# Attention and token mixing on one core: wq and mixing on halves of 288 tokens, bias products 2048 wide, a new order

## The chip, the cores and the metric

One Trainium2 chip, one of its cores. The metric is device microseconds of the whole kernel on that core, the median of several runs. One execution was also taken with the hardware profiler; its trace gives the start and end of every instruction on TensorE (PE), VectorE (DVE), ScalarE (ACT), GpSimd (POOL) and SyncE (SP), and of every DMA.

## What is computed

Eight batches, eight heads, 576 tokens, 64 columns a head. First, attention over a window of 128 tokens with a linear distance bias; then its output, with the heads side by side, is x [576, 512] per batch, and goes through a token mixing layer. q, k, v, the weights and the output are float32 in memory.

```
scores = q @ k^T / 8;  bias = -slope[h] * |i - j|          # 0 <= i - j < 128, else masked
x = softmax(scores + bias) @ v                             # [8, 576, 512]
wq = x @ w_q;  wk = x @ w_k                                # [8, 576, 64]
W_tok = wq @ wk^T / 8
out = relu(W_tok @ x) @ w_out                              # [8, 576, 512]
```

## The kernel before

Every batch goes through the same steps, each a function that the kernel calls once per piece. In the names below b is the batch.

Loads: Lq, Lk (q and k of four heads or of 128 tokens), Lt (the last 64 tokens of two batches), Lv (v of 128 tokens), Lwq, Lwk, Lwo (weights). They stand on POOL's queue and cast to 16 bits (helper line 220); each waits until the loads issued some 6 us of transfer before it have landed (lines 368 to 380). The first half of q comes over SP in 32 bits (FQ) and is cast on an engine (CQ).

Attention: TW, TN and TT transpose q and k on PE into the tile qkT (helper line 217), and ETW, ETN and ETT copy them from PSUM (lines 492, 494, 235, 237). QK{b}.{g}.{u} computes the scores of key group g (128 keys, the last group 192) for four heads u. EXP (line 604, ACT) takes the exponential of 1024 columns from two PSUM banks into the tile pt; MUL (line 611, DVE) multiplies them by the exponential of the bias, which holds the mask too. There are 64 of each. PV{b}.{qt} multiplies by v, with a column of ones for the sum, and X (lines 649 and 650, DVE: a reciprocal and a product) normalises into x; the last 64 tokens of a batch go into xtl.

Mixing: XT transposes x, and EXT copies it (lines 235, 237) into two tiles xT of 256 tokens and a padded one, xTt, of the last 64. WQ computes wq^T from 128 columns of weights, in which the 64 columns of w_q stand twice (tile wqq_sb), so that rows 0 to 63 and 64 to 127 of wqT both hold wq^T: steps .0 and .1 for 256 tokens each, .2 for 64, and EWQ copies each (lines 229, 231). WK gives wk, EWK copies it. G is wk^T x, 64 x 512: columns 0 to 255 of x on one half of the array's columns and 256 to 511 on the other, so that the tile gs holds two halves on rows 0 to 63 and 64 to 127. MX{b}.0 and .1 multiply G^T by wq^T: two matmuls of 512 tokens, each on one half of the array's rows, side by side; .2 does the last 64 tokens in four matmuls. RM is the relu with a scale (line 750 ACT, 752 DVE), per 512 columns, and one of 256 for the tails. OUT multiplies by w_out, four matmuls of 512 columns for 128 tokens; OUT{b}.4, for odd b, does the tails of two batches at once. EO copies the result (229, 231), DO stores it, on POOL or SP (line 223).

All matmuls are recorded at line 214, and all copies at 229, 231, 235 and 237. An array shape stands in the trace as 128*128, 64*128 (row halves) or 128*64 (column halves).

PSUM is four tiles of two banks ("pair"). The order of the work is a table, ORDER: words `name:engine:bank:fills`, from first to last; every engine runs its own words strictly in that order, and waits at a word for what it needs. The fourth field puts that many matmuls on zeros (tile fill, 512 columns) ahead of a step. HOLD marks the place from which stores on SP wait for the last load.

```
EXP0.0.0:A QK0.2.1:P:1:3 QK0.0.1:P:2 QK0.1.1:P:0 MUL0.0.0:V Lv0.1:G EXP0.1.1:A TT0:P:3
...
    for word in ORDER.split():
        name, eng, *rest = word.split(":")
        op = ops.pop(name)
        op.eng = ENG[eng]
...
            op.fill = int(rest[1]) if len(rest) > 1 else 0
```

## Time and profile before

| | before |
|---|---|
| median of 3 runs | 137.87 us (137.78 to 138.77) |
| span of the profiled execution | 137.4 us |
| PE busy | 127.2 us (93%), 2364 matmuls |
| PE weight loads | 83.5 us (61%) |
| DVE busy | 112.0 us (82%), 236 instructions |
| ACT busy | 113.8 us (83%), 187 instructions |
| POOL busy | 105.3 us (77%), 170 instructions |
| mean granted clock of PE | 0.983 |
| last bias product ends | 117.2 us |
| last work of PE | up to 132.5 us |

The profiled execution is one run of its own; its span goes from the first to the last instruction of the core. "Busy" counts an engine's instructions, not its waits, and a busy PE includes the fills. The profile also follows the chain of work that ended last: 72% of the span on PE, 8% on ACT, 5% on loads.

### The profile page before, as it was taken

What the parts mean: (1) busy time and instruction counts of PE and PEld (TensorE: products, weight loads), DVE (VectorE), ACT (ScalarE), POOL (GpSimd) and SP (SyncE); (2) the same over time, 40 slices, a digit from 0 to 9 for tenths busy, and PEclk for the clock granted to TensorE, in tenths of its full rate; (3) what the DMA queues carried; (4) which work ended last, traced back from release to release, by engine and by line L of the source; (5) the groups of instructions that cost most, each with busy time, mean ns of one, the idle gap of its engine ahead of it and who ended that gap; (6) DMA issues with size and microseconds to landing.
All of it is one profiled execution on the core that took longest, in us unless ns stands there. A gap on an engine that the chain in (4) does not pass through costs nothing.

```text
span 137.4 us, 5570 instructions
## 1 busy us (share of the span) xinstructions
PE 127.2 (93%) x2364; PEld 83.5 (61%) x2364; DVE 112.0 (82%) x236; ACT 113.8 (83%) x187; POOL 105.3 (77%) x170
## 2 busy tenths in 40 slices
PE   6997599979999999999999999999999999999950
PEld 2363366778676575667657766766668784765410
DVE  4437838999899999999999999999998899973700
ACT  3769559999979988999989999999999999543750
POOL 6999984899999899999999999999998810100110
PEclk9999959999999999999999999999999999999998
DMA  4999999999999999999999999999999990399994
GB/s 131 162 155 166 158 169 174 181 137 138 135 180 143 163 155 152 149 140 130 143 141 147 149 142 146 140 135 150 198 258 268 342 328 21 115 357 339 329 299 172
DMA packets 92680, 24.86 MB, mean 181 GB/s; under 512 B 80240, under 2 KB 89200, under 8 KB 92656
## 3 DMA queue, kind: packets, MB, share of 16 engines
q0 software_dynamic: 89488, 19.28, 150.0%
q1 hardware_dynamic: 3168, 5.24, 10.8%
q8 instruction: 18, 0.29, 0.8%
q14 instruction: 6, 0.05, 0.1%
HBM read 29.62 MB, written 9.44 MB: 284 GB/s over the span
## 4 chain that ended last, share of the span: by engine, by line
PE 72%; ACT 8%; DMA 5%; POOL 5%; issue 3%; DVE 2%; POOLq 0%; DVEq 0%
PE pair L214 62%; PE pair L217 10%; DMA natw<-in_k_dram 5%; ACT pt L604 5%; POOL natt L220 2%; POOL natw L220 2%; ACT qkT L492 2%; DVE x L650 1%; DVE xtl L650 1%; DVE xT L237 1%; DVE inv L649 0%; ACT xT L235 0%; ACT osb L229 0%; ACT wqT L229 0%; POOL wm L293 0%
## 5 line engine op out<-in xcount | busy, mean ns | idle before, releaser
L604 ACT ACTIVATE pt<-pair 128x1024 f16<-128x1024 f32 x64 | 63.3, 1038 | 6.0 <-PE pair L214 5.8
L220 POOL DMA_DIRECT2D vt<-in_v_dram x40 | 36.5, 968 | 1.2 <-DMA natw<-in_k_dram 0.8
L611 DVE TENSOR_TENSOR pt<-pt,bias 128x1024 f16<-128x1024 f16 x48 | 32.2, 684 | 1.4 <-ACT pt L604 1.3
L214 PE MATMUL pair<-wout_sb,rm 128*128 128x512 f16 x128 | 32.0, 380 | 0.1
L223 POOL DMA_DIRECT2D out_dram<-natw x19 | 10.6, 566 | 19.5 <-DVE natw L231 10.9
L214 PEld LDWEIGHTS <-pt 128*128 128x128 f16 x576 | 21.2, 98 | 5.5 <-issue 2.2
L214 PE MATMUL pair<-qkT 64*128 64x256 f16 (+3 forms) x352 | 23.8, 247 | 0.4 <-ACT pt L604 0.3
L214 PE MATMUL pair<-vt,pt 128*128 128x65 f16 x576 | 23.8, 194 | 0.1
L220 POOL DMA_DIRECT2D natw<-in_k_dram x24 | 22.9, 993 | 1.2 <-POOLq L894 0.8
L220 POOL DMA_DIRECT2D natw<-in_q_dram x23 | 21.5, 989 | 2.0 <-DMA natw<-in_k_dram 0.7
L650 DVE TENSOR_TENSOR x<-pair,inv 128x512 f16<-128x512 f32 x32 | 22.1, 692 | 1.1
L214 PEld LDWEIGHTS <-rm 128*128 128x128 f16 x128 | 10.8, 97 | 10.9 <-issue 0.9
L214 PEld LDWEIGHTS <-qkT 64*128 64x128 f16 x352 | 11.9, 96 | 7.7 <-issue 3.9
L229 ACT COPY natw<-pair 128x512 f32<-128x512 f32 x24 | 14.1, 607 | 2.2 <-PE pair L214 2.1
L217 PEld LDWEIGHTS <-natw 128*64 128x64 f16 (+1 forms) x512 | 12.8, 103 | 4.8 <-issue 1.9
L214 PE MATMUL pair<-fill 128*128 128x512 f16 x28 | 10.4, 506 | 1.2 <-DVE fill L348 1.2
L750 ACT ACTIVATE rm<-pair 128x512 f16<-128x512 f32 x20 | 11.4, 611 | 0.0
L611 DVE TENSOR_TENSOR pt<-pt,biasl 128x1024 f16<-128x1024 f16 x16 | 10.9, 683 | 0.0
L217 PE MATMUL pair<-permh,natw 128*64 128x128 f16 x256 | 9.1, 223 | 1.8 <-DMA natw<-in_k_dram 1.4
L649 DVE RECIPROCAL inv<-pair 128x8 f32<-128x8 f32 (+1 forms) x40 | 8.1, 203 | 3.1 <-PE pair L214 2.3
L214 PE MATMUL pair<-xT,wqq_sb 128*128 128x256 f16 x64 | 9.3, 273 | 0.4 <-ACT qkT L492 0.4
L752 DVE TENSOR_SCALAR rm<-pair 128x512 f16<-128x512 f32 x12 | 7.9, 684 | 1.6 <-PE pair L214 1.6
(76 smaller groups left out, 178.2 us busy)
## 6 DMA issues: line engine op xcount, KB each, us to landing
vt<-in_v_dram POOLq DMA_DIRECT2D x32, 128.0 KB, 5.1
out_dram<-natw POOLq DMA_DIRECT2D x15, 256.0 KB, 5.0
out_dram<-natw SPq DMA_DIRECT2D x13, 256.0 KB, 3.1
natw<-in_k_dram POOLq DMA_DIRECT2D x8, 256.0 KB, 5.6
natw<-in_q_dram POOLq DMA_DIRECT2D x16, 128.0 KB, 5.0
natw<-in_k_dram POOLq DMA_DIRECT2D x16, 128.0 KB, 5.2
natw<-in_q_dram POOLq DMA_DIRECT2D x7, 256.0 KB, 6.0
out_dram<-osb SPq DMA_DIRECT2D x3, 256.0 KB, 3.5
```

The source lines that it names most:

```text
L214: hold(nc.tensor.matmul(*a, **k))
L217: hold(nc.tensor.transpose(*a))
L220: hold(nc.gpsimd.dma_start(**k))
L223: i = (nc.gpsimd if eng == "POOL" else nc.sync).dma_start(**k)
L229: hold(nc.scalar.copy(out_ap, in_ap))
L492: hold(nc.scalar.copy(dst, src))
L604: nc.scalar.activation(out=pt[:, 0:1024], in_=two(s.bank).rearrange("p e c -> p (e c)"), func=AF.Exp, scale=SCALE)
L611: nc.vector.tensor_tensor(out=pt[:, 0:1024], in0=pt[:, 0:1024], in1=bt, op=ALU.mult)
L649: nc.vector.reciprocal(out=inv[r], in_=pxv[r, :, :, 64])
L650: nc.vector.tensor_tensor(out=x[r].rearrange("p (g h d) -> p g h d", g=2, h=4), in0=pxv[r, :, :, 0:64], in1=inv[r].unsqueeze(3).broadcast_ ...
L750: hold(nc.scalar.activation(out=out_ap, in_=in_ap, func=AF.Relu, scale=WSCALE))
L752: hold(nc.vector.tensor_scalar(out=out_ap, in0=in_ap, scalar1=0.0, scalar2=WSCALE, op0=ALU.max, op1=ALU.mult))
```

## The change

1. WQ{b} is one step. It uses the 64 columns of w_q as they are, on column halves: tokens 0 to 287 on one half, 288 to 575 on the other, eight matmuls of 288 columns. wqT then has 288 columns with the token halves on rows 0 to 63 and 64 to 127. It needs all three transposes of x (EXT). The doubled weights and their copy go.
2. G is computed as before, and copied twice: EG into gs as it is, and GX into gx with its halves exchanged (two copies of 64 rows), on ACT in batches 0 and 3, on DVE in batch 7, and by two SP transfers of 64 x 256 elements, from gs, in batches 1, 2, 4, 5 and 6. MX has four steps of two matmuls of 288 columns, on row halves; .2 and .3 use gx. RM takes 2 x 288 columns per step: 32 relus of 576 columns instead of 32 of 512 and 8 of 256. OUT{b}.4 uses column halves, one per batch.
3. xT is one tile of 576 tokens, so that its padded tail tile goes; xtl has four buffers and only their unused halves are set to zero.
4. In batches 1 to 7 one bias product covers both groups of heads, 2048 columns, and waits for both exponentials; batch 0 keeps eight products of 1024. In all 36 products instead of 64.
5. The order is a new one. Fills: 10, all ahead of the first transposes, instead of 28. Several memsets move (ones2, ones4, zerop and pads from POOL to DVE, zerop with five memsets instead of ten), and the casts of the first q are both on DVE. HOLD stands near the end. The helpers' lines shift: 214 is now 207 (matmul), 217 is 210, 604 is 590, 611 is 603, 750 and 752 are 757 and 759.

Words per engine that change most: EO on ACT 27 to 22, on DVE 9 to 14; EXT on ACT 12 to 19, on DVE 12 to 5; RM on ACT 25 to 23, on DVE 15 to 9; EWQ on ACT 14 to 4, on DVE 10 to 4; copies of transposed q and k on ACT 27 to 20, on DVE 13 to 20; DO on POOL 18 to 20, on SP 18 to 16.

```diff
+HS = 288
...
+WIDE = (1, 2, 3, 4, 5, 6, 7)
+DUO = ()
+HW = 2
-PTW = 1088
+PTW = 2112
...
 ORDER = """
-CQ0:V CQ1:A Lt0.2:G zeros:V bias0:A idh:V Lt0.1:G perm:V TW0.0:P:0:12 Lt0.0:G biasl0:V
+Lt0.1:G Lt0.0:G CQ0:V ones2:V CQ1:V perm:V bias0:A TW0.0:P:0:10 ETW0.0.0:A Lt0.2:G zeros:V
...
-    wqq_sb = sb("wqq_sb", [P, 4, P], F16)
...
-    pt_s = [[sb(f"pt{i}{u}", [P, PTW], F16) for u in range(2)] for i in range(NPT)]
+    pt_s = [sb(f"pt{i}", [P, PTW], F16) for i in range(NPT)]
...
-    xT_s = [[sb(f"xT{i}{n}", [P, 4, 256], F16) for n in range(2)] for i in range(2)]
-    xTt_s = [sb(f"xTt{i}", [P, 4, P], F16) for i in range(2)]
-    wqT_s = [sb(f"wqT{i}", [P, S], F16) for i in range(2)]
+    xtl_s = [sb(f"xtl{i}", [P, DM], F16) for i in range(4)]
+    xT_s = [sb(f"xT{i}", [P, 4, S], F16) for i in range(2)]
+    wqT_s = [sb(f"wqT{i}", [P, HS], F16) for i in range(2)]
...
-    rm_s = [[sb(f"rm{i}{c}", [P, DM], F16) for c in range(4)] for i in range(2)]
-    rmt_s = [sb(f"rmt{i}", [P, 4, P], F16) for i in range(2)]
+    gx_s = [sb(f"gx{i}", [P, 256], F16) for i in range(2)]
+    rm_s = [sb(f"rm{i}", [P, 2, 8, HS], F16) for i in range(2)]
...
         x = add(f"EXP{b}.{g}.{u}", ACT(0.905), [s, *oldp], ex, frees=[s])
-        bt = (bias if g < 3 else biasl)[u].rearrange("p e a c -> p (e a c)")
+        wide = b in WIDE
+        exps[b, g, u] = x
+        if wide and u == 0:
+            return
+        us = (0, 1) if wide else (u,)
+        lo, hi = 1024 * us[0], 1024 * us[-1] + 1024
 
         def ml(o):
-            nc.vector.tensor_tensor(out=pt[:, 0:1024], in0=pt[:, 0:1024], in1=bt, op=ALU.mult)
-
-        mul[b, g, u] = add(f"MUL{b}.{g}.{u}", DVE(0.6), [x, (mkb if g < 3 else mkl)[u]], ml)
+            bt = biasw[g == 3].rearrange("p u e a c -> p (u e a c)")
+            nc.vector.tensor_tensor(out=pt[:, lo:hi], in0=pt[:, lo:hi], in1=bt[:, lo:hi], op=ALU.mult)
+
+        m = add(f"MUL{b}.{g}" + ("" if wide else f".{u}"), DVE(1.13 if wide else 0.6),
+                [exps[b, g, v] for v in us] + [(mkb if g < 3 else mkl)[v] for v in us], ml)
+        for v in us:
+            mul[b, g, v] = m
 
...
-    def add_wq(b, i):
-        n = 64 if i == 2 else 256
-
-        def em(o):
-            pw = one(o.bank)
...
+    def add_wq(b):
+        def em(o):
             for c in range(4):
-                rhs = xT_s[b % 2][i][:, c, :] if i < 2 else xTt_s[b % 2][:, c, 64 * (b % 2):64 * (b % 2) + 64]
-                mm(pw[:, 0:n], wqq_sb[:, c, :], rhs, start=(c == 0), stop=(c == 3))
-
-        t = add(f"WQ{b}.{i}", pe(0.436 if i < 2 else 0.116), [wts[0], ext[b, i]], em, banks=1)
-        wqd[b, i] = t
+                for r in range(2):
+                    mm(one(o.bank)[64 * r:64 * r + 64, 0:HS], wq_sb[:, c, :],
+                       xT_s[b % 2][:, c, HS * r:HS * r + HS], start=(c == 0), stop=(c == 3))
+
+        t = add(f"WQ{b}", pe(0.5), [wts[0], *[ext[b, i] for i in range(3)]], em, banks=1, mode=2)
+        wqd[b] = t
 
         def ev(o):
-            cp(o.eng, wqT_s[b % 2][:, 256 * i:256 * i + n], one(t.bank)[:, 0:n])
-
-        old = [mxd.get((b - 2, j)) for j in range(3)]
-        ewq[b, i] = add(f"EWQ{b}.{i}", EV(0.26, 0.34) if i < 2 else EV(0.11, 0.14), [t, *old], ev, frees=[t],
-                        group=f"w{b}")
+            cp(o.eng, wqT_s[b % 2], one(t.bank)[:, 0:HS])
+
+        old = [mxd.get((b - 2, j)) for j in range(4)]
+        ewq[b] = add(f"EWQ{b}", EV(0.292, 0.367), [t, *old], ev, frees=[t])
 
...
-        old = [mxd.get((b - 2, j)) for j in range(3)]
-        egs[b] = add(f"EG{b}", EV(0.26, 0.34), [g, *old], evg, frees=[g])
+        old = [mxd.get((b - 2, j)) for j in range(2)]
+        egs[b] = add(f"EG{b}", EV(0.265, 0.333), [g, *old, gxs.get(b - 2)], evg, frees=[g])
+
+        def evx(o):
+            for r in range(2):
+                out_ap = gx_s[b % 2][64 * r:64 * r + 64, :]
+                lo = slice(64 - 64 * r, 128 - 64 * r)
+                if o.eng == "SP":
+                    hold(nc.sync.dma_start(out=out_ap, in_=gs_s[b % 2][lo, :]))
+                elif o.eng == "POOL":
+                    hold(nc.gpsimd.tensor_copy(out=out_ap, in_=gs_s[b % 2][lo, :]))
+                else:
+                    cp(o.eng, out_ap, one(g.bank)[lo, 0:256])
+
+        old = [mxd.get((b - 2, j)) for j in range(2, 4)]
+        gxs[b] = add(f"GX{b}", {**EV(0.53, 0.666), "POOL": (0.6, 0.65), "SP": (0.9, 0.9)}, [g, egs[b], *old], evx, frees=[g])
 
...
     def add_mix(b, j):
-        g, w = gs_s[b % 2], wqT_s[b % 2]
+        g, w = (gs_s, gx_s)[j // 2][b % 2], wqT_s[b % 2]
 
         def em(o):
             pm = two(o.bank)
-            if j < 2:
-                for r in range(2):
-                    h = slice(64 * r, 64 * r + 64)
-                    mm(pm[:, r, :], g[h, P * j:P * j + P], w[h, 0:512], start=True, stop=True)
+            for r in range(2):
+                h = slice(64 * r, 64 * r + 64)
+                mm(pm[:, r ^ (j // 2), 0:HS], g[h, P * (j % 2):P * (j % 2) + P], w[h, :], start=True, stop=True)
+
+        t = add(f"MX{b}.{j}", pe(0.125, 0.1), [(egs, gxs)[j // 2][b], ewq[b]], em, banks=2, mode=1)
+        mxd[b, j] = t
+        old = [osd.get((b - 4, st)) for st in range(4)]
+        old += [osd.get((b // 2 * 2 - 3, 4))]
+
+        def ev(o):
+            c, n = (2 * j, 5) if j < 2 else (2 * j - 3, 3)
+            relu(o.eng, rm_s[(b // 2) % 2][:, b % 2, c:c + n + 1:n, :], two(t.bank)[:, :, 0:HS])
+
+        erm[b, j] = add(f"RM{b}.{j}", EV(0.532, 0.667), [t, *old], ev, frees=[t], group=f"rm{b}")
+
+    def add_out(b, st):
+        duo = b in DUO and st < 4
+        head = outd.get((b, st - 1)) if duo and st % 2 else None
+
+        def em(o):
+            if head:
+                o.bank = head.bank
+            po = two(o.bank)[:, st % 2, :] if duo else one(o.bank)
+            rm = rm_s[(b // 2) % 2].rearrange("p b c t -> p b (c t)")
+            for db in range(4):
+                if st < 4:
+                    lo = 2 * HS * db + P * st + 64 * (st // 2)
+                    mm(po, rm[:, b % 2, lo:lo + P], wout_sb[:, db, :], start=(db == 0), stop=(db == 3))
+                else:
+                    for e in range(2):
+                        lo = 2 * HS * db + 256
+                        mm(po[64 * e:64 * e + 64], rm[:, e, lo:lo + 64], wout_sb[:, db, :], start=(db == 0), stop=(db == 3))
+
+        need = [*wto]
+        need += [erm[b, db] for db in range(4)]
+        if st == 4:
+            need += [erm[b - 1, db] for db in range(4)]
+        if head:
+            need.append(head)
+        t = add(f"OUT{b}.{st}", pe(0.865, 0.2), need, em, banks=0 if head else 2 if duo else 1, mode=0 if st < 4 else 2)
+        outd[b, st] = t
+        osd[b, st] = t
...
```

PE, the start, before: weight loads and matmuls by turns; the last scores of a step of batch 0 (from qkT_80, its transposed q and k), a fill, and the first transpose of batch 1 (natw_83 is loaded q or k of batch 1, pair_n a PSUM tile).

```order
L214 LDWEIGHTS qkT_80
L214 MATMUL pair_191<-qkT_80 128x256
L214 LDWEIGHTS fill
L214 MATMUL pair_189<-fill 128x512
L217 LDWEIGHTS natw_83
L217 MATMUL pair_189<-permh,natw_83 64x32x4
```

PE, the same place, after: (qkT_77 is the transposed q and k of batch 0, natp_79 loaded q or k of batch 1).

```order
L207 LDWEIGHTS qkT_77
L207 MATMUL pair_159<-qkT_77 128x256
L210 LDWEIGHTS natp_79
L210 MATMUL pair_160<-permh,natp_79 64x32x4
L210 LDWEIGHTS natp_79
```

The fill is gone, and the scores ahead are other ones: the last of key groups 3 and 1 (QK0.3 and QK0.1.1), of which QK0.3 stood behind these transposes before.

ACT, the start, before: constants, then copies of transposed q and k (L492, L235) and exponentials (L604) of batch 0, and from qkT_81 on of batch 1.

```order
L305 ACTIVATE bias_72<-wm 128x256 x4
L492 COPY qkT_80<-pair_189 128x2x256
L604 ACTIVATE pt_147<-pair_190 128x1024
L604 ACTIVATE pt_145<-pair_191 128x1024
L492 COPY qkT_80<-pair_189 128x2x256
L604 ACTIVATE pt_143<-pair_192 128x1024
L604 ACTIVATE pt_146<-pair_189 128x1024
L604 ACTIVATE pt_148<-pair_190 128x1024
L604 ACTIVATE pt_144<-pair_191 128x1024
L235 COPY qkT_80<-pair_192 128x8x32
L604 ACTIVATE pt_149<-pair_190 128x1024
L492 COPY qkT_81<-pair_189 128x2x256 x2
```

ACT, the start, after: the same steps, L478 and L228 for the copies and L590 for the exponentials; qkT_78 is batch 1.

```order
L478 COPY qkT_77<-pair_157 128x2x256
L590 ACTIVATE pt_125<-pair_157 128x1024
L478 COPY qkT_77<-pair_160 128x2x256
L590 ACTIVATE pt_124<-pair_158 128x1024
L590 ACTIVATE pt_124<-pair_157 128x1024
L228 COPY qkT_78<-pair_158 128x8x32
L228 COPY qkT_77<-pair_158 128x8x32
L590 ACTIVATE pt_126<-pair_160 128x1024
L590 ACTIVATE pt_126<-pair_159 128x1024
L590 ACTIVATE pt_127<-pair_157 128x1024
L590 ACTIVATE pt_125<-pair_160 128x1024
L590 ACTIVATE pt_127<-pair_158 128x1024
```

One exponential instead of two stands ahead of the copy of the transposed heads 4 to 7 (the second row with qkT and a PSUM tile of 128x2x256), and all eight exponentials of batch 0 but none of batch 1 stand ahead of the copy of transposed batch 1 of the kind 128x2x256.

DVE, batch 2, before: relus, products (L611), normalisations (L649, L650) and copies.

```order
L611 TENSOR_TENSOR pt_151<-pt_151,bias_72 128x1024
L611 TENSOR_TENSOR pt_146<-pt_146,biasl_75 128x1024
L611 TENSOR_TENSOR pt_145<-pt_145,biasl_74 128x1024
L649 RECIPROCAL inv<-pair_191 128x8
L650 TENSOR_TENSOR x_154<-pair_191,inv 128x512
L611 TENSOR_TENSOR pt_147<-pt_147,bias_72 128x1024
L611 TENSOR_TENSOR pt_149<-pt_149,bias_72 128x1024
L649 RECIPROCAL inv<-pair_192 128x8
L650 TENSOR_TENSOR x_155<-pair_192,inv 128x512
```

DVE, batch 2, after: products are L603, normalisations L644 and L645, copies L224 and L480.

```order
L644 RECIPROCAL inv<-pair_158 128x8
L645 TENSOR_TENSOR x_130<-pair_158,inv 128x512
L224 CAST gs_148<-pair_159 128x256
L603 TENSOR_TENSOR pt_124<-pt_124,bias_72 128x2048
L603 TENSOR_TENSOR pt_125<-pt_125,bias_73 128x2048
L480 TENSOR_SCALAR qkT_78<-pair_157 128x2x256
L644 RECIPROCAL inv<-pair_159 128x8
L645 TENSOR_TENSOR x_131<-pair_159,inv 128x512
L644 RECIPROCAL inv<-pair_158 128x8
L645 TENSOR_TENSOR x_132<-pair_158,inv 128x512
```

A product covers 2048 columns where it covered 1024, and two tiles stand for four.

321 lines of the change are left out of this document (142 added, 179 removed).

## The prediction

> **What bounds the kernel now.** I read the span by stages first, cutting it at the last bias product (117.1 us) and at the end of TensorE's work, then the grouped durations of ScalarE and VectorE, then the timeline at the start and at the end. The columns: stretch, length, busy time (and instructions) of PE, PEld, DVE, ACT and POOL, granted clock, share of the DMA engines, GB/s.
>
> ```profile
> 0.00:9.00 9.00, 7.81 (x55) 3.33 (x57) 4.20 (x22) 4.95 (x11) 7.68 (x17) 1.00 0.99 153
> 9.00:37.00 28.00, 24.55 (x521) 17.70 (x518) 21.99 (x46) 24.58 (x34) 24.63 (x52) 0.94 1.68 155
> 37.00:117.10 80.10, 79.54 (x1610) 53.80 (x1607) 76.45 (x150) 75.62 (x125) 71.31 (x101) 1.00 1.88 170
> 117.10:132.50 15.40, 15.35 (x192) 8.68 (x188) 9.37 (x20) 8.07 (x19) 1.63 (x3) 1.00 0.81 286
> ```
>
> From 37 to 117.1 us three engines are nearly full: TensorE 79.54 of 80.10 (99.3%), VectorE 95.4%, ScalarE 94.4%. TensorE alone is the bound there, with the two others five per cent behind; a gain on it is worth only as much as the next engine lets through. From 117.1 to 132.5 TensorE is full alone. Only before 37 us does it wait. So the sum has four terms: the start, the middle, the stretch behind the last product, the last stores.
>
> **What the change takes from TensorE.** The unit prices, from start to start:
>
> ```profile
> 102.94 0.66 PE L214 MATMUL pair<-vt,pt 128*128 128x65 f16 x16
> 103.46 0.60 PE L214 MATMUL pair<-xT,wqq_sb 128*128 128x256 f16 x4
> 103.89 0.65 PE L214 MATMUL pair<-vt,pt 128*128 128x65 f16 x16
> ...
> 105.24 0.29 PE L214 MATMUL pair<-xTt,wqq_sb 128*128 128x64 f16 x4
> 105.37 0.63 PE L214 MATMUL pair<-wk_sb,xT 128*128 128x64 f16 x16
> ```
>
> ```profile
> 107.77 0.63 PE L214 MATMUL pair<-x,wkn 128*64 128x256 f16 x8
> 108.23 0.28 PE L214 MATMUL pair<-xtl,wkn 128*64 128x256 f16 x2
> 108.44 0.72 PE L217 MATMUL pair<-identh,x 64*128 64x64 f16 x32
> ```
>
> ```profile
> 95.64 1.04 PE L214 MATMUL pair<-wout_sb,rm 128*128 128x512 f16 x4
> 96.51 0.65 PE L214 MATMUL pair<-vt,pt 128*128 128x65 f16 x16
> ...
> 97.65 1.04 PE L214 MATMUL pair<-wout_sb,rm 128*128 128x512 f16 x4
> 98.62 0.26 PE L214 MATMUL pair<-qkT 64*128 64x192 f16 x2
> ```
>
> A whole wq step of four matmuls lasts 103.89 - 103.46 = 0.43 us, the tail's four 0.13 us: 0.99 us per batch. An output step lasts 0.87 us when the next one has the same array shape (96.51 - 95.64) and 0.97 when it has another (98.62 - 97.65), so a change of shape costs 0.10. G, five pairs of matmuls on column halves, takes 0.67 with that 0.10 in it, or 0.114 per pair of 256 columns: the two halves do run side by side. The new wq step is four such pairs of 288 columns, 4 x 0.114 x 288/256 = 0.51 us. That saves 0.48 per batch, 3.8 us over eight. Counted in the instruction order, the shape changes go from 118 to 119 (+0.1); the last output step of a batch pair on column halves costs nothing much (+0.1 for four). Mixing streams 2 x 512 + 128 columns per row half before and 4 x 288 = 1152 after: nothing. TensorE's work without fills falls by 3.6 us.
>
> [...]
>
> Not all of it falls ahead of the last product. Behind that product the list of TensorE held 11 output steps, 4 value steps, 4 wq and 4 mixing steps; now 13, 2, 1 and 7, with ten shape changes for six. By the prices above (value step 0.52, from 102.94 to 103.46; a mixing step 0.12 where it was 0.22, or 0.06 for a tail): +1.74 - 1.04 - 0.61 + 0.30 + 0.40 = +0.8 us for the stretch behind the last product, so TensorE's work in the middle falls by 4.4, to 75.1 us.
>
> **ScalarE and VectorE in the middle.** Here busy time divided by the count is the price, since neighbours overlap a little.
>
> ```profile
> L604 ACT ACTIVATE pt<-pair 128x1024 f16<-128x1024 f32 x64 | 63.3, 1038 | 6.0 <-PE pair L214 5.8
> L229 ACT COPY natw<-pair 128x512 f32<-128x512 f32 x24 | 14.1, 607 | 2.2 <-PE pair L214 2.1
> L750 ACT ACTIVATE rm<-pair 128x512 f16<-128x512 f32 x20 | 11.4, 611 | 0.0
> L235 ACT COPY qkT<-pair 128x512 f32<-128x512 f32 x10 | 5.8, 593 | 0.7 <-ACT wqT L229 0.4 <-PE pair L214 0.3
> ...
> L229 ACT CAST wqT<-pair 128x256 f16<-128x256 f32 x9 | 3.4, 402 | 0.0
> ```
>
> ```profile
> L611 DVE TENSOR_TENSOR pt<-pt,bias 128x1024 f16<-128x1024 f16 x48 | 32.2, 684 | 1.4 <-ACT pt L604 1.3
> ...
> L752 DVE TENSOR_SCALAR rm<-pair 128x512 f16<-128x512 f32 x12 | 7.9, 684 | 1.6 <-PE pair L214 1.6
> L649 DVE RECIPROCAL inv<-pair 128x8 f32<-128x8 f32 x32 | 6.5, 203 | 3.0 <-PE pair L214 2.3
> ```
>
> Counting words of the order up to the last exponential, ScalarE loses five output copies (5 x 0.59 = 2.9), three 512-column and four 256-column transposes (3 x 0.58 + 4 x 0.36 = 3.2), a wk copy and the start's cast (1.1), and its wq copies go from nine of 256 and three of 64 columns to three of 288 (-2.9). It gains five wide and two small copies of xT (+3.5), two copies of G and four half-copies for the swapped G (+2.2), and its relus go from 14 of 512 and 3 of 256 columns to 20 of 576 (+3.0). Sum -1.4, of it 0.6 in the start: 75.62 falls to 74.9 us in the middle. The 64 exponentials, 63.3 us, stay.
>
> VectorE: 64 products become 8 + 28. No wide product stands in the trace. It has as many elements as the two that it replaces, so it saves at least 0 and at most a whole short instruction, the 203 ns of the reciprocal of 8 elements a partition. I take 70 ns, a tenth of a product's 684: 28 x 0.07 = 2.0, bounds 0 and 5.7. Six fewer relus and seven fewer xT copies at 0.68 (-8.8) and six fewer wq copies at some 0.4 (-2.4) stand against five more output copies and six more qkT copies at 0.68 (+7.5). In all 5.7 us less: some 71 us of work in the middle, and not the bound. A product that waits for both exponentials is ready one exponential later than the first of two was, 0.99 us; the value steps behind it in TensorE's list are kept further behind in the new order, and the five buffers of exponentials hide it.
>
> So after the change TensorE holds 75.1 us of work in the middle and ScalarE 74.9: they are level. Neither can be as full as TensorE was alone. Between ScalarE's present share, 94.4%, and TensorE's, 99.3%, I take the middle, 97%: 74.9 / 0.97 = 77.2 us against 80.1, -2.9. Ends: 75.1 / 0.993 = 75.6 (-4.5) and 74.9 / 0.944 = 79.3 (-0.8).
>
> **The start.**
>
> ```profile
> 9.57 1.08 PE L217 MATMUL pair<-permh,natw 128*64 128x128 f16 x32
> ```
>
> ```profile
> 9.14 1.94 ACT L604 ACTIVATE pt<-pair 128x1024 f16<-128x1024 f32 x2 [0.93 <-PE pair L214]
> ...
> 18.87 1.02 ACT L604 ACTIVATE pt<-pair 128x1024 f16<-128x1024 f32 x1 [3.18 <-PE pair L214]
> ```
>
> ```profile
> L220 POOL DMA_DIRECT2D vt<-in_v_dram x40 | 36.5, 968 | 1.2 <-DMA natw<-in_k_dram 0.8 <-DMA natw<-in_q_dram 0.4
> ```
>
> ```profile
> 13.70:17.20 3.50, 2.07 (x41) 1.32 (x41) 2.95 (x6) 2.00 (x3) 3.43 (x7) 0.95 2.08 163
> 17.20:20.60 3.40, 3.38 (x56) 2.24 (x53) 1.14 (x3) 1.73 (x3) 2.92 (x5) 0.55 1.72 168
> ```
>
> ScalarE idles 3.18 us before 18.87, because TensorE's list holds the transposes of batch 1 ahead of the scores of the fourth key block. The new order puts those scores first, and that wait goes. A new one comes: the second exponential stands behind the copy of the transposed heads 4 to 7, whose q is loaded one load later on POOL's queue. The transposes that began at 9.57 end at 10.65, plus about a load's 0.97 is 11.6; the first exponential ends 0.99 after 9.14, at 10.1: a wait of 1.5. The balance is -1.7, against which VectorE gets 21 short memsets and a cast that POOL and ScalarE did, an estimate of 2.5 us at half of the reciprocal's 203 ns for a memset and a wqT copy's 0.38 for the cast; as some lie beside waits I charge half, +1.2. -0.5, bounds -1.7 (all hidden) and +0.7 (none).
>
> Eighteen of 28 fills go. They stand where TensorE waits, so I cost them at nothing as work; their cover of the clock is a rival below.
>
> **Loads and stores.** POOL sheds most of its early memsets, and its loads come no later on the whole. The swapped G goes by SP in five batches, with two copies of 64 partitions each; SP had only stores and the first loads, so the gate on the stores, now near the end, has nothing behind it but stores.
>
> ```profile
> out_dram<-natw SPq DMA_DIRECT2D x13, 256.0 KB, 3.1
> ...
> 131.37 2.06 SPq L223 DMA_DIRECT2D out_dram<-osb  x3
> ```
>
> The nearest row is a store of 256 KB, 3.1 us from issue to landing. The tightest use is batch 2, where three output steps, one value step and two score steps stand between G and the first mixing step that needs it: 3 x 0.87 + 0.52 = 3.1 us and the scores. That just covers such a transfer, and I take 0; if the cover fails, up to 1 us. The last store is the two-batch tail in two halves on SP, whose three last stores took 2.06 us, 0.69 each: +0.4, bounds 0 and 0.7.
>
> Sum: -0.5 - 2.9 + 0.8 + 0.4 = -2.2. The profiled execution's span is 137.4 and the median of the runs 137.87, 0.4 more; 135.2 becomes 135.6 us.
>
> **Rivals.**
> B, everything packs: TensorE stays at 99.3% of a shorter list. For it: it did so with the others at 95%. Against it: ScalarE, at 74.9 us, has 0.2 us of slack, not 4. Middle -4.5, else as above: -3.8, 134.0; with the start at -1.7, 132.8.
> C, the engines go on waiting for each other: ScalarE stays at 94.4% of its own work, and TensorE's saving becomes waits for exponentials and relus. For it: the exponentials already waited 6.0 us for TensorE. Middle -0.8, sum -0.1: 137.7, no difference.
> D, the clock falls in the start: at 13.7 to 17.2 us TensorE was busy 2.07 of 3.50 us, and in the next 3.4 us its granted clock was 0.55. With the fills gone an earlier stretch may look like that one; a transpose step of 1.1 us then takes twice that, and three of them stand on the chain in the start: +3.3, 138.9, slower than before. It decides from a loss of 2.2 us on, two such steps. Against it: ahead of the first transposes ten fills remain, and the scores follow each other more closely than before.
> [...]
>
> **How the numbers follow.** My forecast 0.45, B 0.18, C 0.20, D 0.15, anything else 0.02. One per cent, 1.4 us, is about what a measurement can tell from no change. Faster by more than that (below 136.5): B and four fifths of the forecast, 0.56 with the rest; within it: C, the rest of the forecast and a third of D, 0.34; slower (above 139.2): two thirds of D, where C comes on top, 0.10. The range goes from B's low end, 132.8, to D, 138.9.
>
> **What would show it.** The wq step at 0.5 us instead of 0.43 + 0.43 + 0.13; the last product some 3.4 us earlier than 117.1; ScalarE's idle time before exponentials shorter than 6.0 us in sum, with no single wait of 3 us in the start; a clock of 1.00 from 10 to 20 us; wide products under 1.3 us each. It is wrong if TensorE's busy share in the middle falls below 95% (then C), if the granted clock shows 0.5 before 20 us for longer than now (D), or if mixing steps on the swapped G wait for an SP transfer.

## The result, and the profile after

The change is slower. Its median is 145.59 us (144.31 to 149.14, four runs) against 138.32 us (137.78 to 140.26) of the kernel before in the same series: 1.048 times as long, interval 1.039 to 1.058. A second series gave 145.12 us, 1.046 (1.039 to 1.053). Some executions are disturbed and run longer, the first profiled one (149.14 us) among them, so medians here are of all runs, ratios and intervals of the undisturbed ones alone, and the lines below are of a run of the second series, 145.12 us with a span of 142.9.

Two tables by stage, first the change, then the kernel before in the one stretch that both spend in full work. Columns: stretch, length, busy time (and instructions) of PE, PEld, DVE, ACT and POOL, granted clock, share of the DMA engines, GB/s.

```profile
span 142.9 us, 5486 instructions
...
9.00:40.00 31.00, 24.65 (x514) 19.69 (x515) 24.29 (x62) 25.37 (x36) 25.72 (x39) 0.83 1.77 164
40.00:115.00 75.00, 71.09 (x1516) 48.39 (x1515) 68.14 (x112) 69.58 (x106) 64.16 (x83) 1.00 1.88 159
...
120.00:138.20 18.20, 17.90 (x183) 9.11 (x181) 12.62 (x24) 7.55 (x14) 4.48 (x9) 1.00 0.77 275
138.20:142.90 4.70, 0.05 (x2) 0.00 (x0) 0.00 (x0) 0.59 (x1) 0.00 (x0) 0.74 0.54 168
```

```profile
40.00:115.00 75.00, 74.73 (x1505) 50.54 (x1503) 71.86 (x142) 71.32 (x116) 68.41 (x88) 1.00 1.96 174
```

On the average of 40 to 115 us neither TensorE nor ScalarE nor VectorE is full in the changed kernel: TensorE 94.8% (before 99.6%), ScalarE 92.8% (95.1%), VectorE 90.9% (95.8%). The average hides a stretch in which ScalarE is, from 50 to 60 us (10.00 of 10.00, where it had 8.68 before); the change first, then before:

```profile
50.00:60.00 10.00, 9.55 (x201) 6.53 (x198) 9.23 (x17) 10.00 (x15) 8.98 (x12) 1.00 2.04 151
```

```profile
50.00:60.00 10.00, 10.00 (x234) 6.53 (x229) 9.48 (x20) 8.68 (x15) 10.00 (x13) 1.00 2.32 150
```

TensorE is nearly full again behind the last product (17.90 of 18.20 us), which ends at 120.2 us instead of 117.2.

What TensorE waits for between 40 and 115 us, in the change (waiting engine and its line, engine and line waited for: us in total, times, longest us); the kernel before has no such row above 0.2 us there.

```profile
PE pair L207 <- ACT qkT L228: 1.2, 2, 0.7
PE pair L207 <- DMA gx<-gs: 0.9, 2, 0.7
...
PE pair L210 <- ACT pt L590: 0.7, 2, 0.4
...
PE pair L210 <- DVE x L645: 0.4, 1, 0.4
...
PE pair L210 <- DVE xtl L645: 0.3, 1, 0.3
```

No single wait stands out: eight waits under 0.8 us, for five different producers, 3.5 us of the 3.9 that TensorE idles. The engines waited for wait for TensorE in their turn, in the same stretch:

```profile
DVE inv L644 <- PE pair L207: 2.1, 4, 1.0
...
ACT rm L757 <- PE pair L207: 1.7, 3, 1.1
ACT pt L590 <- PE pair L207: 1.7, 5, 0.5
...
DVE qkT L230 <- PE pair L210: 1.3, 2, 0.8
```

**An account of TensorE's losses.** Idle time misses the steps that start but run slowly. So I give each step its price between neighbours of its own shape, plus 0.10 us for a change of shape (an output step took 0.97 us with one behind it and 0.87 without, before), and take the sum of the steps begun by a time t from t. That is what TensorE has lost by then (worked out from the trace, us):

| | by 20 | by 40 | by 60 | by 80 | by 100 | by 120 | end | TensorE's work | its end |
|---|---|---|---|---|---|---|---|---|---|
| before | 14.0 | 17.5 | 17.9 | 18.6 | 19.3 | 20.0 | 20.2 | 112.3 | 132.5 |
| the change | 14.3 | 19.8 | 22.9 | 25.4 | 27.0 | 28.4 | 29.0 | 109.3 | 138.2 |

The span grew by 5.5 us: TensorE's work -3.0, loss up to 40 us +2.3, loss behind it +6.5 (9.2 against 2.7), last stores -0.3 (4.7 us instead of 5.0). By 60 us eight output steps were begun before, two now; by 100 us 21 and 15. The exponentials were not late by 60 us, 33 done against 32, but the last ends at 118.9 us instead of 114.6.

**The start.** The granted clock, in stretches of 3.4 us, first the change and then before:

```profile
6.80:10.20 3.40, 0.87 (x27) 0.79 (x23) 1.87 (x15) 1.04 (x3) 3.30 (x11) 1.00 1.66 157
10.20:13.60 3.40, 2.62 (x46) 2.20 (x42) 1.46 (x9) 2.12 (x3) 2.75 (x4) 0.58 1.49 160
13.60:17.00 3.40, 1.70 (x52) 1.29 (x46) 2.55 (x6) 3.10 (x6) 2.60 (x3) 0.92 1.55 162
17.00:20.40 3.40, 2.74 (x44) 2.25 (x40) 2.68 (x6) 3.40 (x5) 2.15 (x5) 0.58 2.13 165
20.40:23.80 3.40, 2.38 (x36) 1.98 (x38) 2.88 (x7) 1.58 (x3) 3.06 (x5) 0.50 1.48 166
23.80:27.20 3.40, 2.91 (x64) 2.23 (x61) 2.37 (x5) 2.75 (x4) 2.61 (x4) 0.91 1.80 156
```

```profile
6.80:10.20 3.40, 3.40 (x64) 2.05 (x60) 1.20 (x3) 2.21 (x5) 3.40 (x6) 1.00 1.70 157
10.20:13.60 3.40, 2.63 (x46) 1.40 (x40) 2.38 (x5) 3.31 (x5) 3.22 (x13) 1.00 1.46 158
13.60:17.00 3.40, 1.87 (x39) 1.24 (x41) 2.96 (x7) 2.10 (x3) 3.23 (x7) 0.98 2.11 162
17.00:20.40 3.40, 3.38 (x52) 2.12 (x48) 1.03 (x4) 1.53 (x3) 2.92 (x5) 0.52 1.73 173
20.40:23.80 3.40, 3.09 (x78) 2.30 (x75) 3.01 (x7) 3.40 (x5) 1.89 (x3) 1.00 1.39 171
23.80:27.20 3.40, 3.40 (x93) 2.71 (x91) 3.26 (x7) 3.39 (x6) 2.63 (x4) 1.00 1.55 184
```

In the change TensorE is busy 0.87 of 3.40 us up to 10.2, and the clock is about half in three of the next four stretches; before, in one. The cause of that gap is on VectorE. Its own list, then TensorE's (start, length, instruction, in brackets the idle time before it and what ended it):

```profile
8.05 0.55 DVE L324 MEMSET qkT<- 128x256 uint32 x2 [1.88 <-ACT qkT L478]
8.69 0.28 DVE L316 MEMSET vt<- 64x264 uint32 x1
9.06 0.07 DVE L318 MEMSET vt<- 128x8 f16 x1
9.08 0.70 DVE L480 TENSOR_SCALAR qkT<-pair 128x512 int32<-128x512 int32 x1
```

```profile
9.84 0.86 PE L207 MATMUL pair<-qkT 64*128 64x256 f16 x12 [2.53 <-DVE qkT L480]
```

The step "zeros" clears a part of qkT. In the new order it stands behind the first transposes, shares a tile with ScalarE's copy of them, and waits 1.88 us for that copy; the copy of the second half of the heads (line 480) stands behind it and behind a memset of v. So the first scores wait 2.53 us, for two memsets that nobody needed yet.

A second such place comes later. The memset of xtl, which the change took from POOL to VectorE, stands ahead of another copy that scores wait for (VectorE, then TensorE):

```profile
19.46 1.36 DVE L332 MEMSET xtl<- 64x256 uint32 x4
20.74 0.62 DVE L480 TENSOR_SCALAR qkT<-pair 128x512 int32<-128x512 int32 x1
```

```profile
21.42 1.04 PE L207 MATMUL pair<-qkT 64*128 64x256 f16 x8 [1.17 <-DVE qkT L480]
```

The account sets a limit to the first wait: by 20 us the change has lost 14.3 us and the kernel before 14.0, so the 2.53 us are nearly made up by then. The 2.3 us more by 40 us come mostly behind 20 us, with the clock at half up to 24.4 (worked out from the 0.91 behind 23.80).

### The profile page after: what moved, and what is told of

Same layout as the page of the kernel before. It is cut to its first block, busy times and chain, and to the rows that moved or that the text cites. A ratio compares the mean times of both kernels' runs of the same rounds, so it can differ in the third digit from the quotient of the medians.

```text
span 146.9 us, 5486 instructions
## 1 busy us (share of the span) xinstructions
PE 126.7 (86%) x2330; PEld 84.7 (58%) x2330; DVE 113.7 (77%) x223; ACT 112.5 (77%) x173; POOL 102.5 (70%) x147
## 4 chain that ended last, share of the span: by engine, by line
PE 65%; ACT 13%; DVE 8%; DMA 7%; issue 4%; DVEq 0%; ACTq 0%; POOLq 0%
PE pair L207 54%; PE pair L210 11%; ACT pt L590 8%; DMA natp<-in_k_dram 4%; DMA gx<-gs 3%; DVE x L645 2%; DVE qkT L480 1%; ACT qkT L228 1%; ACT qkT L478 1%; DVE xtl L645 1%; DVE inv L644 1%; ACT rm L757 1%; DVE xtl L332 1%; DVE gx L224 1%; DVE rm L759 1%
## 5 line engine op out<-in xcount | busy, mean ns | idle before, releaser
L590 ACT ACTIVATE pt<-pair 128x1024 f16<-128x1024 f32 x64 | 63.4, 1044 | 7.6 <-PE pair L207 7.4
L603 DVE TENSOR_TENSOR pt<-pt,bias 128x2048 f16<-128x2048 f16 (+1 forms) x36 | 38.9, 1098 | 1.0 <-ACT pt L590 0.8
L207 PE MATMUL pair<-wout_sb,rm 128*128 128x512 f16 (+1 forms) x160 | 35.7, 381 | 0.0
L216 POOL DMA_DIRECT2D out_dram<-natp x19 | 10.7, 566 | 20.6 <-DVE natp L224 15.1
L645 DVE TENSOR_TENSOR x<-pair,inv 128x512 f16<-128x512 f32 x32 | 22.1, 691 | 1.1
L213 POOL DMA_DIRECT2D natp<-in_k_dram x24 | 21.8, 929 | 1.1 <-POOLq L909 0.8
L213 POOL DMA_DIRECT2D natp<-in_q_dram x23 | 20.6, 917 | 0.3 <-issue 0.2
L207 PEld LDWEIGHTS <-rm 128*128 128x128 f16 (+1 forms) x160 | 12.4, 100 | 13.1 <-issue 1.9
L210 PEld LDWEIGHTS <-natp 128*64 128x64 f16 (+1 forms) x512 | 15.9, 114 | 6.4 <-issue 4.7
L757 ACT ACTIVATE rm<-pair 128x576 f16<-128x576 f32 x23 | 14.7, 662 | 4.2 <-PE pair L207 3.9
L222 ACT COPY natp<-pair 128x512 f32<-128x512 f32 x19 | 11.2, 601 | 7.3 <-PE pair L207 7.1
L210 PE MATMUL pair<-permh,natp 128*64 128x128 f16 x256 | 11.4, 255 | 1.6 <-DVE permh L279 0.7
L644 DVE RECIPROCAL inv<-pair 128x8 f32<-128x8 f32 (+1 forms) x40 | 8.1, 203 | 4.8 <-PE pair L207 3.8
L228 ACT COPY xT<-pair 128x512 f32<-128x512 f32 (+1 forms) x19 | 8.9, 481 | 3.5 <-PE pair L210 3.2
L224 DVE COPY natp<-pair 128x512 f32<-128x512 f32 x13 | 8.9, 689 | 2.3 <-PE pair L207 2.2
L478 ACT COPY qkT<-pair 128x512 f32<-128x512 f32 x9 | 5.4, 616 | 3.4 <-PE pair L210 3.4
```

Source lines behind the costliest of these rows:

```text
L207: hold(nc.tensor.matmul(*a, **k))
L210: hold(nc.tensor.transpose(*a))
L213: hold(nc.gpsimd.dma_start(**k))
L216: i = (nc.gpsimd if eng == "POOL" else nc.sync).dma_start(**k)
L222: hold(nc.scalar.copy(out_ap, in_ap))
L224: hold(nc.vector.tensor_copy(out=out_ap, in_=in_ap))
```

## The experiments

The question was which of the parts costs what: the start, the transfer of the swapped G, the wide products, or the order as a whole.

**First group: the start, the fills, the transfer.** Four kernels. The first moves the memsets back out of the way:

```diff
-dist:V idh:V ones4:V
+dist:V idh:V zeros:V
...
-Lk1.0:G ones0:V ETW0.0.1:V zerop:V
+Lk1.0:G ETW0.0.1:V ones0:V zerop:V
...
-EXP0.3.0:A pads:V
+EXP0.3.0:A ones4:V pads:V
```

> The changed kernel, with only the early memsets on VectorE in another order: the zeros of the padding of qkT ahead of the first transposes, ones0 behind the second copy of transposed q and k (ETW0.0.1), ones4 later. Theory S (start): in the profile of the change the first scores wait 2.53 us for that copy, which stands behind a memset that itself waited 2.21 us; TensorE idles, and its clock stays at half from 8.5 to 26 us. Without that wait the first scores come some 2.5 us earlier and the clock stays full: 145.1 falls to about 139.5, granted clock above 0.98. Rival M (middle): the loss comes from waits of the new order behind 35 us, and the start is caught up there: 144 to 145. In between, the wait goes but the clock still falls: 142.5 to 143.5.

Measured: 146.07 us, ratio to before 1.050 (1.041 to 1.059), no gain over the change. The edit did what it was for, and no more. TensorE's list in this kernel:

```profile
8.17 0.86 PE L207 MATMUL pair<-qkT 64*128 64x256 f16 x12 [1.04 <-ACT qkT L478]
10.65 1.79 PE L210 MATMUL pair<-permh,natp 128*64 128x128 f16 x32 [1.62 <-DMA natp<-in_q_dram]
```

The first scores start 1.67 us earlier than at 9.84, but the next transposes start at 10.65, as in the change (10.62): now they wait for the load of q. And ones4 and pads (the memset of xtl), which now stand together, delay a copy of batch 1. The account gives 20.7 us lost by 40 us, against 19.8. So the wait of 1.88 us alone is not what costs in the start.

The second kernel keeps the clock up: banks 0 and 1 swapped, so that fills can stand ahead of steps where TensorE waits.

```diff
-QK0.1.0:P:0
+QK0.1.0:P:1:10
...
-TW0.1:P:3
+TW0.1:P:3:3
```

> The changed kernel with its late memset left as it is, PSUM pairs 0 and 1 exchanged behind the first transposes, and 10 fills ahead of the first scores and 3 ahead of the second transposes, on free banks: TensorE is busy in the wait. Nothing else moves. If the clock, and not the lateness, is what costs (S, clock part): the first scores still start 2.5 us late, but the clock stays at 1.0 beyond 10 us, and the time falls by 3 to 4 us to 141 to 142. If the lateness alone costs, or the middle (M): no difference, 144.5 to 145.5.

Measured: 144.27 us, 1.038 (1.030 to 1.047). The timed runs had a mean granted clock of 0.984 to 0.988, where the change has 0.946 to 0.97. So the clock comes back, and with it some 1 us; the intervals overlap, and the size isn't settled. The half clock isn't what costs 7 us.

The third takes the swapped G away from SP, on top of the first: its copies go to ScalarE (batches 1, 4, 6) and VectorE (2, 5).

```diff
-GX1:S
+GX1:A
...
-GX2:S
...
+EG2:A GX2:V
```

> As the kernel with the memsets mended, and the swapped G copied from PSUM by ScalarE (batches 1, 4, 6) and VectorE (2, 5) directly behind G's own copy, no SP transfer. If the SP transfer is a wait on the way to the end (mixing steps waited 1.9 us for it in the profile of the change, the chain names it with 3%): 1 to 2 us less than the kernel with the memsets alone. If the wait is taken up by other waits, or ten more half-copies on two full engines cost as much: within 0.7 us of it, or slower.

Measured: 149.74 us, 1.081 (1.073 to 1.088), 3.7 us more than the first. The transfer costs TensorE 0.9 us in the table of waits above; with ten more copies on the engines that TensorE waits for, the kernel loses four times that. The transfer's own waits explain little of the 7 us; this run can't show more, since it puts other work in its place.

The fourth is the kernel before, with its fills cut from 28 to the 10 ahead of the first transposes:

```diff
-TW0.0:P:0:12
+TW0.0:P:0:10
...
-QK0.2.1:P:1:3
+QK0.2.1:P:1
```

> The kernel before with its 28 fills cut to the 10 ahead of the first transposes, as the change has it, and nothing else. If the fills are what keeps the clock (rival D of the prediction): about +3.3 us, 141.5, with a granted clock of 0.5 for several us more before 25 us. If the fills only fill waits: 138, within 0.5 us of before; a cold stretch of one window more would show as +1 to +2.

Measured: 138.72 us, 1.002 (0.998 to 1.007), the same. In the order of before, the eighteen fills are worth nothing: they cost nothing as work, and their removal lowers the mean granted clock only from 0.99 to 0.98 (medians of the runs), without a loss of time.

**Second group: the parts and the order.** Two kernels with all the parts of the change, but in the order of before, each new step put at the earliest place where its inputs are ready; the second has narrow products. In both of these the bank of PSUM of one output step (OUT0.0) is overwritten by a mixing step (MX1.2) before it is copied, so some values of the result are wrong; the steps are the same, and the wait for that one copy is missing.

```diff
-WQ0.0:P:20
...
-WQ0.1:P:21
+WQ0:P:21
...
-WQ0.2:P:31
...
-EG4:V
+EG4:V GX4:S
```

> All parts of the change (wq in one step on column halves, four mixing steps, swapped G, wide products) in the order of the kernel before, its 28 fills and memsets kept: the one wq step stands at the later of the two old wide ones, the mixing steps .2 and .3 between the two relus of each old PSUM pair, a wide product at the later of the two old ones. Theory O (the new order costs, the parts don't): at or below before, 136 to 138.5, since TensorE has about 2.5 us less work. Rival P (the parts cost: halves, swapped G, wide products): 142 to 146, as the change.

> As the kernel with all parts in the order before, but with 64 products of 1024 columns at their old places: the wq and mixing part alone. Theory O: 135.5 to 138. If the wide products are what costs (each waits for two exponentials and holds VectorE 1.2 us): 2 to 5 us less than the kernel with all parts. If halves and swapped G cost: 141 or more.

Measured: 166.45 us, 1.202 (1.194 to 1.210), and 163.07 us, 1.166 (1.156 to 1.175). With the old order the parts are 17 to 20% slower, not faster. Two rows of the waits of the narrow one, over its whole span, show a large part of it:

```profile
PE pair L211 <- DMA gx<-gs: 8.8, 4, 3.3
...
ACT rm L761 <- PE pair L211: 20.7, 14, 4.0
```

Mixing steps on the swapped G stand there right behind G and wait up to 3.3 us for the transfer, and the relus wait for them. These two kernels, put together by one rule, can't tell the price of the parts from that of the order.

The third is the kernel before with only the wide product of batches 1 to 7, at the place of the later of the two narrow ones:

```diff
-EXT0.2:A MUL1.0.1:V EXP1.2.0:A
+EXT0.2:A EXP1.2.0:A
...
-TW2.0:P:1 MUL1.0.0:V Lt1.2:G
+TW2.0:P:1 MUL1.0:V Lt1.2:G
```

> The kernel before with wide products in batches 1 to 7 at the later of the two old places, and nothing else. By the prediction a wide product saves 0.07 us and its wait is hidden: 137 to 138.5. If waiting for both exponentials is not hidden: 140 to 143.

Measured: 146.01 us, 1.042 (1.032 to 1.051). The wide product alone, in the order of before, costs as much as the whole change. The change itself ran beside it as a control:

> The changed kernel unchanged, beside the others on one chip, for a second profile: 144 to 146. Every theory says the same.

Measured: 145.12 us, 1.046 (1.039 to 1.053); its profile stands above.

**Third group: length or place?** A wide product is one long instruction, and it starts later than the first narrow one did. The kernel before with its narrow products, but the first of each pair moved to directly ahead of the second, has the place without the length. 28 instructions move, nothing else:

```diff
-EXT0.2:A MUL1.0.1:V EXP1.2.0:A
+EXT0.2:A EXP1.2.0:A
...
-TW2.0:P:1 MUL1.0.0:V
+TW2.0:P:1 MUL1.0.1:V MUL1.0.0:V
```

> The kernel before with its narrow products, but the first of each pair in batches 1 to 7 moved directly ahead of the second, where the wide one stood in the kernel before with wide products (146.0). It waits no longer for one long instruction, only for its place in the order. If the place (behind both exponentials) is what cost there: 143 to 147. If the length of the instruction, 1.2 us that hold VectorE, or the merged tile: 138 to 140.

Measured: 145.84 us, 1.049 (1.042 to 1.057): the whole cost with none of the length. Its engines from 40 to 115 us, and under them those of the kernel before with wide products:

```profile
40.00:115.00 75.00, 70.85 (x1421) 47.08 (x1414) 66.94 (x131) 66.46 (x106) 67.89 (x87) 1.00 1.95 167
```

```profile
40.00:115.00 75.00, 71.73 (x1448) 48.04 (x1443) 66.35 (x112) 67.52 (x110) 67.91 (x87) 1.00 1.95 171
```

Both look like the change: TensorE at 94.5% and 95.6%, the others below it. The granted clock is 1.00 in these stretches. And the waits of the kernel with late narrow products, 40 to 120 us, and under them ScalarE's in the kernel before:

```profile
ACT pt L600 <- PE pair L210: 4.0, 9, 0.6
...
DVE inv L645 <- PE pair L210: 2.5, 6, 0.8
...
PE pair L210 <- DVE x L646: 1.4, 3, 0.7
...
PE pair L210 <- DVE pt L607: 0.6, 2, 0.4
```

```profile
ACT pt L604 <- PE pair L214: 1.6, 5, 0.6
```

As in the change, the engines wait for each other in a ring. I read it so: a product that waits for the second exponential lets the value steps start late (DVE pt), the normalisation waits for these (DVE inv), the transposes of x wait for it (DVE x), and with TensorE's list held up the next scores, so the next exponentials, come late too (ACT pt: 4.0 us, where the kernel before has 1.6 us). The account shows it behind 40 us, not in the start:

| | by 40 us | end | behind 40 us |
|---|---|---|---|
| before | 17.5 | 20.2 | 2.7 |
| before, wide products | 16.3 | 25.0 | 8.7 |
| before, narrow products late | 16.4 | 26.4 | 10.0 |
| the change | 19.8 | 29.0 | 9.2 |

If that were the cause in the new order too, narrow products with the first at its own exponential should free it. In this kernel the first product of each of the 28 pairs goes to the place in VectorE's list where its exponential has ended in the trace of the change:

```diff
-WIDE = (1, 2, 3, 4, 5, 6, 7)
+WIDE = ()
...
-PV0.1:P:2 ETW1.1.1:V
+PV0.1:P:2 MUL1.0.0:V ETW1.1.1:V
...
-Lk2.0:G MUL1.1:V MUL1.0:V
+Lk2.0:G MUL1.1.1:V MUL1.0.1:V
```

> The changed kernel with 64 products of 1024 columns: the first of each pair at the place on VectorE where its exponential ends in the second profile of the change, the second where the wide one stood; all else as it is. Theory W (the wide products are what costs in the middle, as they cost 5% in the order before): 139 to 142. Rival L (with TensorE, ScalarE and VectorE level, the losses are spread over all steps, and the products are not the cause): 144.5 to 147, as VectorE gets up to 28 x 0.13 us more work.

Measured: 151.38 us, 1.092 (1.084 to 1.100), slower by 6 us than the change. So in the new order this edit does not free it. That the wait for both exponentials costs nothing there is not shown, since this order was not made for narrow products and 28 more instructions of VectorE stand in it.

A first mended start, with loads and memsets as before and eight fills, alone and with the narrow products:

```diff
-Lk0.0:G ident:G iota:G dist:V idh:V ones4:V Lk0.1:G mask:G Lq0.1:G bias1:A
+Lk0.0:G iota:G Lq0.1:G dist:V mask:G Lk0.1:G ident:G idh:V zeros:V bias1:A
...
-QK0.1.0:P:0
+QK0.1.0:P:1:5
```

> The changed kernel with its start mended as a whole: early memsets off the path of the copies (zeros first, ones4 and pads behind the first normalisations), POOL's first loads in the order of the kernel before, PSUM pairs 0 and 1 exchanged and 5 and 3 fills ahead of the first scores and the second transposes. TensorE had lost 2.3 us more than before by 40 us. Theory S: it carries to the end: 142 to 143. If the stages behind absorb it, as they did for the memsets alone: 144.5 to 146.

> Both: start mended and narrow products. If both theories (S and W) hold: 136.5 to 139, at or below the kernel before. If only S: 142 to 144; if neither: 144.5 to 147.

Measured: 149.74 us, 1.070 (1.060 to 1.080), and 156.51 us, 1.127 (1.118 to 1.136). The mending failed, and usefully. TensorE's list:

```profile
8.02 1.92 PE L210 MATMUL pair<-permh,natp 128*64 128x128 f16 x32 [2.38 <-DVE permh L279]
9.87 2.31 PE L207 MATMUL pair<-fill 128*128 128x512 f16 x5
```

The identity, moved behind the loads, came late, the first transposes waited for it and took 1.92 us (1.08 in the change), and five fills took 2.31 us there instead of covering a wait. The account has 22.9 us lost by 40 us, 3.1 more than the change, and 32.2 at the end, 3.2 more. The 3.1 us lost more in the start of this order are still lost at the end.

**Fourth group: the waits themselves.** Three kernels: six TensorE steps moved by one to three places at the longest waits behind 40 us; a second mended start (perm and zeros first, ones4 and pads behind the second normalisation, ones0 behind the copy that the scores need; a load, the second transposes of batch 1 and two copies earlier); both together. The diff shows two places of the second.

```diff
-X1.3:V XT1.2:P:30
+X1.3:V XT1.0:P:0 XT1.2:P:30
...
-EXT2.2:V TN4.1.0:P:3 QK3.2.0:P:1
+EXT2.2:V QK3.2.0:P:1 TN4.1.0:P:3
...
-TN4.0.1:P:0 Lv4.4:G
+TN4.0.1:P:0 MX2.1:P:3 MX2.3:P:1 Lv4.4:G
```

> The changed kernel with six steps of TensorE's list moved by one to three places, at the longest waits behind 40 us: XT1.0 ahead of XT1.2, the scores QK3.2.0 ahead of TN4.1.0, mixing steps .1 and .3 of batch 2 behind TN4.0.1, the scores QK5.0.1 behind the value step PV4.0, OUT3.4 ahead of QK6.0.0. Each of these waits (0.4 to 0.8 us, 3.5 us in all) stands where a step follows the step that makes its input with no other step between. Theory N (the new order stands such pairs next to each other, and their latency is TensorE's loss): 141.5 to 143. If what is saved there is lost at the next wait, since the other engines set the pace: 144.5 to 145.5.

```diff
-idh:V ones4:V Lk0.1:G mask:G Lq0.1:G
+idh:V perm:V zeros:V Lk0.1:G Lq0.1:G mask:G
...
-X0.1:V EXP1.1.1:A
+X0.1:V ones4:V pads:V EXP1.1.1:A
```

> The changed kernel with its start mended without fills: perm and zeros directly behind the identity, ones4 and pads behind the second normalisation, ones0 behind the second copy, Lq0.1 ahead of the mask, the second half of the bias behind the first copy, the tails' copies ahead of an exponential, and the second transposes of batch 1 ahead of its first scores. Theory S: TensorE, which had lost 19.8 us by 40 us against 17.5 before, loses 2 to 3 us less there, and that carries to the end, as the loss of 3.1 us did in the first trial of a mended start: 142 to 143. If the stages behind absorb it: 144.5 to 145.5.

> Both edits together. If both theories hold, the gains add: 139 to 140.5, within 1.5% of the kernel before. If one holds: 142 to 143. If the pace is that of the other engines: 144 to 145.5.

Measured: 146.66 us, 1.049 (1.041 to 1.057); 146.08 us, 1.053 (1.047 to 1.059); 145.93 us, 1.049 (1.043 to 1.056). None differs from the change. The second start has the loss of the change by 40 us, 19.8 us. In the last one the waits that were aimed at are gone or shorter, but others stand in their place, and they come to 3.6 us in all from 40 to 120 us, as in the change. Two of the largest, and the stage:

```profile
PE pair L207 <- DMA gx<-gs: 1.2, 1, 1.2
PE pair L210 <- ACT pt L590: 0.7, 2, 0.4
```

```profile
40.00:115.00 75.00, 71.11 (x1516) 48.67 (x1514) 67.68 (x112) 69.31 (x106) 63.52 (x82) 1.00 1.86 155
```

71.11 us of TensorE against 71.09: these edits moved the waits and did not lessen them. The exponentials show an unchanged pace behind them: the 32nd, the 40th and the last end at 56.6, 75.0 and 118.8 us with the mended start alone, and at 56.6, 74.8 and 118.9 in the change.

**Fifth group: the backlog of output steps.** Six output steps fewer are done by 60 us than before, and they come back as work at the end. Two kernels put the four output steps of batch 0 earlier (in the first of them three start some 3 us earlier and one 13 us), with the loads of w_out earlier and a mixing step of batch 2 later, one with the second start in it. The diff shows some of the places:

```diff
-Lwo.1:G Lk4.0:G
+Lwo.1:G Lwo.3:G Lwo.2:G Lwo.0:G Lk4.0:G
...
-XT2.2:P:20 EXT2.2:V TN4.1.0:P:3
+XT2.2:P:20 OUT0.0:P:21 EXT2.2:V EO0.0:V TN4.1.0:P:3
...
-WK2:P:20 QK3.1.0:P:3
+WK2:P:20 OUT0.1:P:21 QK3.1.0:P:3
```

> The changed kernel with the four output steps of batch 0 some 6 us earlier on TensorE (behind XT2.2, WK2, WQ2 and TN4.0.0, on banks that are free there), the last three loads of w_out ahead of Lk4.0, and the first mixing step on the swapped G of batch 2 behind PV3.3. Theory I (the new order puts output steps off: by 60 us 2 of 36 are done, before 8, while ScalarE is 97% full; TensorE loses 3 us there and has that work left when it is the bound, from 62 us on): 142 to 143.5. If it is the pace of ScalarE and VectorE, 97% and 95% full in that stretch, that decides, the four copies push the exponentials back by as much: 144.5 to 146.

> The same, with the second trial of the mended start. Theory I with a start that now can be used, since TensorE has work to run: 140.5 to 142. If only I: 142 to 143.5. If neither: 144.5 to 146.

Measured: 148.57 us, 1.064 (1.054 to 1.073), and 148.01 us, 1.063 (1.056 to 1.069): slower than the change. From 60 to 70 us, this kernel and then the change:

```profile
60.00:70.00 10.00, 7.43 (x118) 4.30 (x111) 8.38 (x12) 7.39 (x12) 10.00 (x13) 1.00 2.24 148
```

```profile
60.00:70.00 10.00, 9.05 (x186) 5.82 (x184) 8.02 (x16) 8.28 (x14) 10.00 (x13) 1.00 2.32 153
```

The steps moved forward push the scores back; ScalarE then has 7.39 us to do instead of 8.28. The 32nd exponential ends at 59.1 us instead of 56.6, and the last at 122.3.

## Why the prediction was wrong

Against the forecast, up to the last product: -3.4 us predicted, +3.0 measured. Behind it +0.8 predicted, +2.8 measured; last stores +0.4 and -0.3.

**The step that failed is the middle: "between ScalarE's present share, 94.4%, and TensorE's, 99.3%, I take the middle, 97%".** It took the busy time of the fullest engine as the length of the stage, short of a packing of 97%. In 40 to 115 us none of the three came above 94.8%. TensorE's work ahead of the last product did fall, by some 5 us; its losses between 40 and 120 us went from 2.5 to 8.6 us, which eats all of it. The share of 99.3% was no property of the engine, but of one order, in which TensorE has no wait above 0.2 us from 40 to 115 us; with another order and other dependencies it had to be found anew, and the old share said nothing of it. The rival of engines that go on waiting for each other named the mechanism, and the mark that it gave (TensorE's share under 95%) is in the trace, if only just; but it bounded the price by the old share of ScalarE, and that fell as well.

**A second step that failed is "the five buffers of exponentials hide it"**, said of the product that waits for both exponentials. In the order of before this place alone makes the kernel 1.049 times as long (1.042 to 1.057), with narrow products and the same work. That is shown for the order of before. For the new one it isn't: there narrow products at the earlier place made it slower.

**The start**, -0.5 predicted, +2.3 measured. The forecast counted the memsets that VectorE gets as work, at half their price, and did not ask what stands behind them in the queue: one waits 1.88 us for a copy on another engine, and another of 1.36 us stands ahead of a copy that TensorE waits for. That is the step that failed here, but it does not account for the +2.3: with the first memset moved 20.7 us are lost by 40 us, and with both moved (the second mended start) 19.8 us, as in the change. Other waits take their place, so the cause of the +2.3 stays open. The prediction also said that the loads "come no later on the whole". By count that holds (35 have landed by 40 us, 34 before), but single ones are later: the second half of batch 0's q, for which the second transposes wait, lands at 10.2 us instead of 8.0. The chain that ended last runs over loads and POOL up to 38.9 us in the change, and leaves the loads at 16.3 before; the last load on it, here and before:

```profile
34.58 4.30 DMA vt<-in_v_dram
```

```profile
9.12 7.13 DMA natw<-in_k_dram
```

A new order with the loads in the places of before was not tried on its own. The rival of a falling clock named the right place, but with the wrong cause: without the fills the kernel before is the same (1.002), and in the change half clock stands behind stretches in which TensorE has gaps (busy 0.87 and 1.70 of 3.40 us, then 0.58 each). With fills ahead of the first scores and the second transposes the mean clock of the runs is 0.984 to 0.988, where the change has 0.946 to 0.97. The half clock is worth some 1 us, not settled. An estimate from the rows of the start, with the clock taken as either full or half: half for 3.4 us in all before, and for 3.4 and then 6.9 us in the change.

**TensorE's work**, -3.6 predicted, -3.0 measured. The wq step is right (0.49 to 0.51 us measured, 0.51 predicted). The changes of shape were mis-sized: counted step by step they go from 108 to 118, ten more at 0.10 us each; the 118 to 119 of the forecast had the fills' shape among them, and fills that go took their changes with them. The tail's output step on column halves is as priced: the next step, of another shape, starts 0.96 to 0.99 us after it, as behind a full one (0.97).

**Behind the last product**, +0.8 predicted, +2.8 measured: 18.1 us instead of 15.3. Fourteen output steps stood there, not thirteen, against eleven before, at 0.87 us each; a mixing step on the last swapped G waits 0.3 us more, by the trace for a relu on VectorE. The rest is not broken down.

**What was right, and nearly.** The fills cost nothing. The swapped G was taken at 0, with up to 1 us if its cover fails: it failed, with 0.9 us of waits, so the bound held and not the term. The old wait of 3.18 us in ScalarE's start is gone, and the new one of 1.5 us is 1.20; but the first exponential waits 2.34 us for its scores, where it waited 0.93. And the wide product saves time on VectorE, more than I took:

```profile
L603 DVE TENSOR_TENSOR pt<-pt,bias 128x2048 f16<-128x2048 f16 x28 | 33.6, 1217 | 0.1
```

28 of them take 33.6 us, 1.20 each; two narrow ones took 2 x 32.2/48 = 1.34. That is 0.14 us for a pair, 4.0 us in all where the forecast had 2.0, on an engine that was not the bound.

**What stays open.** The losses behind 40 us are 6.5 us larger than before. Shown is that the fills do not make them in the old order, that the SP transfer's waits are 0.9 us of them, that moving the longest single waits takes nothing off, and that in the old order the later place of 28 products makes about as much, with long and with short instructions. What sets the pace of the new order isn't settled: ScalarE, full from 50 to 60 us, is one candidate, and the loads of the start are another; the parts in the old order are slower still, with waits for the transfer, and an order made for the parts without the wide products was not tried.
